# Probabilities turned in 32x32 blocks on VectorE and through DRAM in place of most TensorE transposes

## The chip, the cores and the metric

One core of a Trainium2 chip runs the whole program. The metric is the device time in microseconds, the median of the runs shown; lower is better.

## What is computed

Three stages, each on the output of the one before, all in float32 with 4 batches of 576 positions:

```python
# 1. attention, 8 heads of 64, each position sees itself and the 63 before it
scores = scale * q @ k^T;  attn = softmax(where(0 <= i - j < 64, scores, -1e9))
x = (attn @ v)                       # 4 x 576 x 512
# 2. gated layer with a spatial mix
h = relu(x @ w_in);  u, v = halves of h
v_s = w_spatial @ layernorm(v) + b_spatial
x = (u * v_s) @ w_out
# 3. four attention experts, causal, the best two per position by x @ w_gate
for e in range(4):
    a = softmax(causal(scale * (x @ wq[e]) @ (x @ wk[e])^T))
    out += gate[e] * (a @ (x @ wv[e])) @ wo[e]
```

## The kernel before, in words

A planner in the kernel file sets the order of all work. Each step is a node made with `N((engine, ns), emit, deps, alloc, use)`; `Planner.run` (L224) goes through time with the costs written at the nodes, gives each free engine the ready node with the lowest key and emits it at once. So each engine executes a fixed order, and at run time it waits in that order for the semaphores of what a step needs. The keys are one number per node in the long table `KEY` (L39), not derived from the node. When TensorE would go between full 128x128 products and the products on parts of its array, `SWITCH` is added to the key (L252). DMAs are nodes of SP (`load`, L511) and go through one hardware queue in order.

There are two planned phases.

Phase 1 holds stages 1 and 2. The first attention is done in 24 couples (`a_couple`, L581), a couple being two groups of 192 positions of a head pair. Per couple, TensorE makes the scores (`s_mm`, L612) into two PSUM banks, one for each head of the pair, each of three 128x128 blocks. Per bank, VectorE adds the mask and takes the extremum (L629), ScalarE does the exponential and the sum (L635), VectorE the reciprocal (L653), VectorE, GpSimd or ScalarE the scaling (L641, L643). Then TensorE transposes P three times (`p_t`, L647), a copy moves it from PSUM into `pt` (L656), and `pv` (L669) multiplies with V. The rings `pa` and `pt` hold four tiles of one head's P each (L497, L500). The second stage (`b_v`, `b_u`, `b_mix`) is woven between the couples: the first batch's couples run mostly ahead of it, those of the later batches beside it.

Phase 2 is the third stage. For each batch and each of two expert pairs, 8 pairs in all, `scores` (L1226) makes the causal scores of the query tiles I = 0 to 3 (128 I + 128 keys wide; 0 and 1 together) and of the tail tile 4. `unit` (L1278) does for one tile and one expert the mask and extremum (L1307), exponential (L1313), reciprocal (L1316) and scaling by the gate (L1317), then I + 1 transposes (`tr`, L1327) and a copy into `pg` (`tc_`, L1331). `c_pv` (L1351) multiplies with V, once for tiles 0 and 1 (group 0) and once for tiles 2 to 4 (group 1). `c_wo` (L1391) projects and stores. P tiles are five of 128x576 (L1070); projections of the next pair (`c_qk`, `c_v`) and the output projection are woven between the units (L1456 to L1466).

The masks are made at the start on VectorE and GpSimd (L450 to L470). Products of TensorE with an identity keep it busy at the start and wherever nothing else is ready (L515 to L523, 68 of them).

Of the kernel before, what the change touches and what calls it, by code (L numbers as in the profile page):

```python
# [8 lines left out]
F32 = mybir.dt.float32  # L9
# [13 lines left out]
N_XT = 5  # L23
N_VR = 3
N_W2 = 2
N_Q = 6
SWITCH = (51316.5562883, 56444.76665)
A_BIAS = 10098.0
C_BIAS = 162315.0
DVE_BIAS = (924.812225719, 2809.18155958)  # L30
POOL_BIAS = (605.73769693, 3223.06614942)
# [3 lines left out]
EFT = (348.130120865, 591.3127716)  # L35
# [6 lines left out]
    1e+09, 1e+09, 1e+09, 1e+09, 1e+09, 1e+09, 1e+09, 1e+09, 1e+09, 1e+09, 1e+09, 1e+09, 1e+09, -433949.337, -310768.212, -410360.675, -53326.873, -46012.043, -29718.587, 29893.476, 36423.798, 130640.442, 48760.892, -102410.634,  # L42
# [136 lines left out]
class Planner:  # L179

    LAT = 200.0, 165.0, 130.0, 75.0, 900.0
    ISSUE, WAY, RATE, FLIGHT = 475.0, 650.0, 360.0, 8

    DRAIN = (0.0, 145.0, 145.0, 92.0), (0.0, -78.0, 0.0, 0.0), (0.0, 0.0, -78.0, 0.0), (0.0, 0.0, 0.0, -92.0)

    CLASH, BEHIND = 1.0, 2200.0

    def __init__(self):
        self.nodes, self.free, self.prio = [], [1500.0, 2000.0, 2900.0, 7600.0, 560.0], 0.0
        self.moved, self.unit = [-1e9] * self.FLIGHT, 0
# [158 lines left out]
def attn_gmlp_moe_kernel(ctx: ExitStack, tc: tile.TileContext, kq0, qT, kT, v, w_in, wspT, b_sp, w_outT,  # L352
# [110 lines left out]
    for x in range(2):  # L463
        MASK[x, 1 - x] = m = const.tile([128, 128], F32, name=f"mix{x}")
        for y in range(2):
            pool.tensor_scalar(m[HALF[y]], (mask0, mask1)[x ^ y][HALF[y]], 1.0, 1.0, op0=ALU.mult, op1=ALU.mult)
# [757 lines left out]
    SC = {}  # L1224
# [292 lines left out]
```

## Time and profile before

| | us |
|---|---|
| median of 3 runs | 441.62 |
| lowest to highest | 441.45 to 443.12 |
| the profiled execution | 441.42 |
| its span, first to last instruction | 439.6 |
| TensorE products busy | 432.1 |
| VectorE busy | 288.6 |
| ScalarE busy | 275.8 |
| GpSimd busy | 90.0 |

Busy times are added over the span. The time of an execution holds some 1.8 us around its span. A float32 product is recorded as two instructions, a transpose as one. PEld is TensorE's loading of its stationary operand, which runs beside its products. An engine's idle time is put down to what it waited for last.

### The profile page before, as it was taken

What the parts mean: (1) busy time and instruction counts of PE and PEld (TensorE: products, weight loads), DVE (VectorE), ACT (ScalarE), POOL (GpSimd) and SP (SyncE); (2) the same over time, 40 slices, a digit from 0 to 9 for tenths busy, and PEclk for the clock granted to TensorE, in tenths of its full rate; (3) what the DMA queues carried; (4) which work ended last, traced back from release to release, by engine and by line L of the source; (5) the groups of instructions that cost most, each with busy time, mean ns of one, the idle gap of its engine ahead of it and who ended that gap; (6) DMA issues with size and microseconds to landing.
All of it is one profiled execution on the core that took longest, in us unless ns stands there. A gap on an engine that the chain in (4) does not pass through costs nothing.

```text
span 439.6 us, 10921 instructions
## 1 busy us (share of the span) xinstructions
PE 432.1 (98%) x4058; PEld 390.0 (89%) x4058; DVE 288.6 (66%) x1238; ACT 275.8 (63%) x883; POOL 90.0 (20%) x132
## 2 busy tenths in 40 slices
PE   8999999999999999999999999999999999999997
PEld 7988989998889989998999999999799978987775
DVE  4999998695787583354435444977654956498750
ACT  4899986787785273352433352867576748557873
POOL 4556754121041050001100120120012101110000
PEclk9999999999999999999999999999999999999999
DMA  8995614364145020121001000000020002000114
GB/s 269 339 343 151 238 51 154 96 205 120 38 108 147 1 73 0 49 73 49 1 1 50 0 1 1 0 2 2 1 97 1 1 1 98 1 0 2 49 51 143
DMA packets 31079, 33.11 MB, mean 75 GB/s; under 512 B 1905, under 2 KB 24689, under 8 KB 31026
## 3 DMA queue, kind: packets, MB, share of 16 engines
q1 hardware_dynamic: 31026, 32.41, 23.5%
q8 instruction: 32, 0.52, 0.5%
q14 instruction: 21, 0.17, 0.1%
HBM read 27.68 MB, written 4.72 MB: 74 GB/s over the span
## 4 chain that ended last, share of the span: by engine, by line
PE 84%; DVE 10%; ACT 3%; issue 1%; DMA 1%; POOL 1%; SPq 0%; DVEq 0%; POOLq 0%; ACTq 0%
PE bank L416 75%; PE bank L1329 5%; PE bank L647 4%; DVE p L1307 3%; DVE p L1300 2%; DVE p L1317 1%; ACT p L1313 1%; DMA kt<-in_kT_dram 1%; POOL p L1317 1%; DVE mc L1315 1%; DVE qk L440 0%; DVE mc L1316 0%; ACT pa L635 0%; DVE t2w L440 0%; DVE pa L629 0%
## 5 line engine op out<-in xcount | busy, mean ns | idle before, releaser
L416 PE MATMUL bank<-xh,w 128*128 128x288 f32 x512 | 109.5, 298 | 0.0
L416 PEld LDWEIGHTS bank<-xh,w 128*128 128x128 f32 x512 | 84.1, 188 | 1.4 <-issue 0.3
L416 PE MATMUL bank<-xl,w 128*128 128x288 f32 x256 | 75.5, 295 | 0.0
L416 PE MATMUL bank<-w,xh 128*128 128x512 f32 (+1 forms) x256 | 64.8, 343 | 0.0
L635 ACT ACTIVATE pa<-pa,mx 128x128 f32<-128x128 f32 x144 | 55.8, 393 | 12.7 <-DVE mx L629 12.6
L1313 ACT ACTIVATE p<-p,mc 128x256 f32<-128x256 f32 (+4 forms) x72 | 41.5, 577 | 15.5 <-DVE mc L1307 13.7
L416 PEld LDWEIGHTS bank<-xl,w 128*128 128x128 f32 x256 | 48.1, 188 | 0.4
L416 PEld LDWEIGHTS bank<-w,xh 128*128 128x128 f32 x256 | 43.0, 188 | 5.0 <-DVE mx L651 0.2
L416 PE MATMUL bank<-w,xl 128*128 128x512 f32 (+1 forms) x128 | 43.2, 338 | 0.0
L1317 POOL TENSOR_SCALAR p<-p,mc,fx 128x384 f32<-128x384 f32 (+4 forms) x22 | 14.6, 664 | 133.8 <-DVE mc L1316 66.8
L416 PE MATMUL bank<-wsp_h,vh 128*128 128x288 f32 x128 | 38.9, 304 | 0.0
L416 PE MATMUL bank<-wsp_l,vh 128*128 128x288 f32 x128 | 37.7, 294 | 0.0
L416 PE MATMUL bank<-wsp_h,vl 128*128 128x288 f32 x128 | 37.7, 294 | 0.0
L1307 DVE CUSTOM_DVE_ANT_0 p<-bank,cmask 128x512 f32<-128x512 f32 (+3 forms) x64 | 28.8, 487 | 4.8 <-PE bank L416 2.4
L629 DVE CUSTOM_DVE_ANT_0 pa<-bank,mask 128x128 f32<-128x128 f32 x120 | 28.2, 286 | 4.4 <-PE bank L416 4.3
L853 POOL TENSOR_TENSOR st<-st,nhalf 128x1 f32<-128x1 f32 (+1 forms) x20 | 11.8, 592 | 92.2 <-DVE st L852 56.6
L427 ACT ACTIVATE pg<-bank 128x512 f32<-128x512 f32 (+4 forms) x80 | 29.7, 438 | 0.7 <-PE bank L1329 0.2
L1329 PE MATMUL bank<-ident,p 128*128 128x128 f32 x192 | 27.2, 276 | 1.7 <-DVE p L1317 0.7
L427 ACT ACTIVATE pt<-bank 128x384 f32<-128x384 f32 x41 | 18.4, 486 | 15.8 <-PE bank L647 15.8
L635 ACT ACTIVATION_READ_ACCUMULATOR pa<-pa,mx 128x1 f32 x144 | 27.6, 192 | 0.0
L416 PEld LDWEIGHTS bank<-w,xl 128*128 128x128 f32 x128 | 24.1, 188 | 2.8
L1329 PEld LDWEIGHTS bank<-ident,p 128*128 128x128 f32 x192 | 21.6, 140 | 5.5 <-DVE p L1317 2.6
(193 smaller groups left out, 989.9 us busy)
## 6 DMA issues: line engine op xcount, KB each, us to landing
vt<-in_v_dram SPq DMA_DIRECT2D x12, 512.0 KB, 5.0
qa<-in_qT_dram SPq DMA_DIRECT2D x44, 96.0 KB, 4.4
out_dram<-ot SPq DMA_DIRECT2D x15, 256.0 KB, 2.1
y<-in_w_in_dram SPq DMA_DIRECT2D x7, 512.0 KB, 6.2
kt<-in_kT_dram SPq DMA_DIRECT2D x12, 288.0 KB, 5.3
y<-in_w_outT_dram SPq DMA_DIRECT2D x4, 512.0 KB, 4.2
y<-in_wspT_dram SPq DMA_DIRECT2D x2, 576.0 KB, 4.0
vt<-in_kq_dram SPq DMA_DIRECT2D x2, 384.0 KB, 3.8
```

The source lines that it names most:

```text
L416: pe.matmul(o, lhsT, rhs, start=start, stop=stop)
L427: act.activation(o, i, AF.Copy)
L629: dve.tensor_tensor_reduce(out=pa[:, j, :], in0=ps[:, j * 128:(j + 1) * 128], in1=mask(j), scale=-0.125, scalar=3.0e38, op0=ALU.add, op1=A ...
L635: act.activation(pa[:, j, :], pa[:, j, :], AF.Exp, bias=mx[:, j, 0:1], scale=-1.0, accum_out=mx[:, j, 1:2])
L647: pe.transpose(ps2[:, j * 128:(j + 1) * 128], pa[:, j, :], ident)
L853: a = N((POOL, 464), lambda e: pool.tensor_tensor(out=st[:m, 9:10], in0=st[:m, 8:9], in1=nhalf[:m], op=ALU.pow), [n1], use=[st])
L1300: dve.tensor_tensor_reduce(out=P[HALF[y], a0:a1], in0=ps[y][HALF[y], :HS], in1=cmask[HALF[y], 0:HS] if i == 0 else tmask[HALF[y]], scale=- ...
L1307: tops = [N((DVE, t_tt(L)), lambda _, ps=ps: dve.tensor_tensor_reduce(out=P[:, cs], in0=ps[:, cs], in1=cmask[:, 512 - L:512], scale=-0.125 ...
L1313: a = N((ACT, 284 + 0.87 * L), lambda e: act.activation(P[:, cs], P[:, cs], AF.Exp, bias=mc[:, 0:1], scale=-1.0, accum_out=mc[:, 2:3]), to ...
L1315: a = N((DVE, 70), lambda e: dve.tensor_scalar(mc[:, 3:4], mc[:, 2:3], 1e-9, None, op0=ALU.add), [a], use=[mc], prio=prio)
L1317: a = N({POOL: 328 + 0.832 * L, DVE: 90 + 0.52 * L}, lambda e: engs[e].tensor_scalar(P[:, cs], P[:, cs], mc[:, 3:4], fx[:, I, ev:ev + 1], ...
L1329: pe.transpose(ps[:, j * m:(j + 1) * m], P[:, c0 + j * 128:c0 + (j + 1) * 128], ident)
```

## The change

P of the last 16 couples of the first attention (`far`, from group 16 on) and of tiles 0 to 3 of all expert pairs but the last, (3, 1), is transposed in another way. The mask step writes P with its columns sorted by 32-column blocks; one VectorE instruction turns all 32x32 blocks of a tile in place; four DMAs write the four 32-partition strips to a DRAM tile, and a read (one, or two where a tile's experts lie apart) brings them back so that keys lie on partitions. The transposes on TensorE and the copies out of PSUM go for these. Near couples, the last pair and every tail tile keep them.

For this the P tiles become 128x768 for both heads of a couple (`pa` 4, `pt` 3 instead of 4) and 128x1024 in the second attention (6 instead of 5); `pg` is laid out in blocks of 32 queries; the scores' keys of far pairs are read in sorted order; the product with V of group 0 goes tile by tile. A mask `kmask` with sorted columns is made by GpSimd at the start. The tail tile's copy is split in two. The planner gets a table of the cost of going from each of five forms of product to each other one (transposes form a form of their own), other costs for some nodes, and a new `KEY` for every node. The program is built with a DMA scratch of 2048.

```diff
-SWITCH = (51316.5562883, 56444.76665)
+N_DT = 16
+NEAR = {(3, 1)}
+N_P = 6
+SWITCH = (508440.848706, 3824.76008776)
...
-    DRAIN = (0.0, 145.0, 145.0, 92.0), (0.0, -78.0, 0.0, 0.0), (0.0, 0.0, -78.0, 0.0), (0.0, 0.0, 0.0, -92.0)
+    DRAIN = ((0.0, 138.0, 137.0, 191.0, 0.0),
...
-                    key = n.prio + (SWITCH[self.phase] if e == PE and (n.form > 0) != (self.form > 0) else 0.0), n.nth
+                    key = n.prio + (SWITCH[self.phase] * self.DRAIN[self.form][n.form] if e == PE else 0.0), n.nth
...
+    for I in range(4):
+        L, c = 128 * I + 128, 64 * I * I + 64 * I
+        pool.tensor_copy(kmask[:, c:c + L].rearrange("p (k j c) -> p k j c", k=4, c=32),
+                         cmask[:, 512 - L:512].rearrange("p (j k c) -> p k j c", k=4, c=32))
...
-    r_pa = ring(p1, "pa", [128, 3, 128], F32, 4)
+    r_pa = ring(p1, "pa", [128, 768], F32, 4)
-    r_pt = ring(p1, "pt", [128, 3, 128], F32, 4)
+    r_pt = ring(p1, "pt", [128, 768], F32, 3)
+    r_dr = ring(dram, "dr", [4, 4, 32, 192], F32, 4)
...
+        far = n0 >= N_DT
...
+        if far:
+            a = N((DVE, 870), lambda e: dve.transpose(pa.t, pa.t), done, use=[pa], prio=prio, sbuf=True)
+            dr = r_dr.new()
+
+            def there():
+                for i in range(4):
+                    dma(dr[i].rearrange("k a w -> a k w"), pa[i * 32:(i + 1) * 32, :].rearrange("p (k w) -> p k w", k=4))
+
+            a = load(128 * 3072, 4, there, [a], alloc=[dr], use=[pa], prio=prio)
+            done = [load(128 * 3072, 1, lambda: dma(pt.t.rearrange("p (i w) -> p i w", i=4),
+                                                    dr.t.rearrange("i k a w -> (k a) i w")), [a], alloc=[pt], use=[dr], prio=prio)]
...
-                        mm(ps3[HALF[e], (3 * x + j) * 64:(3 * x + j + 1) * 64], vap(x, vi, e), pts[e][:, j, HALF[x]])
+                        mm(ps3[HALF[e], (3 * x + j) * 64:(3 * x + j + 1) * 64], vap(x, vi, e), prob(j, x, e))
...
-    r_p = Ring(None, 5, tiles=[p2.tile([128, S], F32, name=f"p{i}") for i in range(5)])
+    r_p = Ring(None, N_P, tiles=[p2.tile([128, 1024], F32, name=f"p{i}") for i in range(N_P)])
+    r_d2 = ring(dram, "d2", [4, 4, 32, 256], F32, 8)
...
+                return x.rearrange("p (j k c) -> p k j c", k=4, c=32) if perm else x
...
+    def far(b, pr, tiles):
+        prio = plan.prio - C_BIAS
+        scores(b, pr, tiles, prio)
+        w = sum(64 * I + 64 for I in tiles)
...
+        a = N((DVE, 68 + 4.16 * w), lambda e: dve.transpose(P[:, :4 * w], P[:, :4 * w]), done, use=[P], prio=prio, sbuf=True)
+        d2, grp = r_d2.new(), int(tiles[0] > 1)
...
+        def there():
+            for i in range(4):
+                dma(d2[i, :, :, :w].rearrange("k a w -> a k w"), P[i * 32:(i + 1) * 32, :4 * w].rearrange("p (k w) -> p k w", k=4))
+
+        def back():
+            src = d2[:, :, :, :w].rearrange("i k a w -> (k a) i w")
+            if grp == 0:
+                dma(pg.t, src)
+            elif w == 256:
+                dma(pg[:, 4:8].rearrange("p i e c -> p i (e c)"), src)
+            else:
+                for e in range(2):
+                    dma(pg[:, 0:4, e, 0:96], src[:, :, 96 * e:96 * e + 96])
...
+                    if grp == 0:
+                        for i in range(j, 2):
+                            c = 64 * i + e * 32 * (i + 1) + 32 * j
+                            mm(ps[e * 64:(e + 1) * 64, i * 128:(i + 1) * 128], v2[:, j, vs], pg[:, :, c:c + 32], j == 0, j == i)
+                        continue
+                    if j < 4:
+                        x = pg[:, a // 32:, e, j * 32:j * 32 + 32]
...
+        if (b, pr) not in NEAR:
+            us = [(1700, lambda: far(b, pr, [0, 1])), (760, lambda: c_pv(b, pr, 0)), (1200, lambda: far(b, pr, [2])),
+                  (1600, lambda: far(b, pr, [3])), (1600, lambda: unit(b, pr, 0, 4)), (2420, lambda: c_pv(b, pr, 1))]
+            return us
...
-    nc = _bacc.Bacc("TRN2", target_bir_lowering=False, num_devices=1)
+    nc = _bacc.Bacc("TRN2", target_bir_lowering=False, num_devices=1, dynamic_dma_scratch_size=2048)
```

## Rows read from the trace of the kernel before

**Rows 1.** Page, parts 1 and 2: busy time by engine; granted clock in 40 slices.
```profile
PE 432.1 (98%) x4058; PEld 390.0 (89%) x4058; DVE 288.6 (66%) x1238; ACT 275.8 (63%) x883; POOL 90.0 (20%) x132
...
PEclk9999999999999999999999999999999999999999
```
**Rows 2.** Busy time by stretch: from:to, length, each engine (instructions), clock, DMA share, GB/s.
```profile
0.00:66.00 66.00, 63.53 (x752) 56.46 (x756) 57.05 (x242) 56.24 (x192) 38.73 (x63) 1.00 0.71 232
66.00:200.00 134.00, 134.00 (x1460) 123.30 (x1453) 88.72 (x395) 83.03 (x306) 26.21 (x32) 1.00 0.30 87
...
275.00:430.00 155.00, 153.28 (x1264) 132.86 (x1261) 107.59 (x510) 105.81 (x314) 17.61 (x24) 1.00 0.06 22
```
**Rows 3.** Page, part 4: the chain that ended last, by engine.
```profile
PE 84%; DVE 10%; ACT 3%; issue 1%; DMA 1%; POOL 1%; SPq 0%; DVEq 0%; POOLq 0%; ACTq 0%
```
**Rows 4.** The same stretches, instructions on tile pt alone: PE, PEld, DVE, ACT.
```profile
66.00:200.00 134.00, 14.05 (x384) 12.24 (x384) 1.64 (x3) 12.91 (x29) 1.00 0.30 87
```
**Rows 5.** TensorE in order of time: start, duration, products around three transposes, first stage.
```profile
195.78 0.29 PE L416 MATMUL bank<-t1w,t1v 128*128 128x288 f32 x1
195.91 0.29 PE L416 MATMUL bank<-t2w,t2v 128*128 128x288 f32 x1
196.04 0.49 PE L647 MATMUL bank<-ident,pa 128*128 128x128 f32 x3
...
196.51 0.29 PE L416 MATMUL bank<-wsp_l,vh 128*128 128x288 f32 x1
```
**Rows 6.** TensorE in order of time around eight transposes, second attention.
```profile
346.71 0.30 PE L416 MATMUL bank<-xh,w 128*128 128x288 f32 x1
346.85 1.03 PE L1329 MATMUL bank<-ident,p 128*128 128x128 f32 x8
...
347.85 0.30 PE L416 MATMUL bank<-xl,w 128*128 128x288 f32 x1
```
**Rows 7.** Groups by line and shape: count, busy us, mean ns, idle before and its releasers.
```profile
L1329 PEld LDWEIGHTS bank<-ident,p 128*128 128x128 f32 x192 | 21.6, 140 | 5.5 <-DVE p L1317 2.6 <-POOL p L1317 1.5 <-DVE mc L1315 0.8
...
L427 ACT ACTIVATE pg<-bank 128x512 f32<-128x512 f32 x24 | 14.0, 597 | 0.4
...
L427 ACT ACTIVATE ot<-bank 128x512 f32<-128x512 f32 x17 | 9.9, 591 | 5.5 <-PE bank L416 4.3 <-ACT pg L427 0.8 <-ACT xh L427 0.5
...
L440 DVE TENSOR_TENSOR xl<-y,xh 128x576 fp32r<-128x576 f32 x10 | 7.9, 813 | 3.6 <-ACT xh L427 3.4
...
L416 PE MATMUL bank<-qk 64*128 64x512 f32 x48 | 7.2, 403 | 0.0
...
L1317 DVE TENSOR_SCALAR p<-p,mc,fx 128x512 f32<-128x512 f32 x13 | 7.1, 543 | 0.1
...
L757 POOL TENSOR_SCALAR y<-y 128x512 f32<-128x512 f32 x5 | 3.9, 786 | 2.9 <-DMA y<-in_w_in_dram 2.1 <-DVE wol L440 0.6 <-POOL woh L429 0.2
...
L416 PE MATMUL bank<-qk 64*128 64x128 f32 x48 | 3.8, 263 | 0.0
...
L440 DVE TENSOR_TENSOR w<-vt,w 128x1024 fp32r<-128x1024 f32 x3 | 3.7, 1226 | 1.1 <-ACT w L427 0.9
...
L440 DVE TENSOR_TENSOR wsp_l<-y,wsp_h 128x576 fp32r<-128x576 f32 x3 | 3.4, 1149 | 0.1
```
**Rows 8.** The stretch from 275 us, instructions on tile pg alone: PE, PEld, ACT, POOL.
```profile
275.00:430.00 155.00, 22.54 (x216) 13.95 (x216) 29.72 (x80) 0.00 (x0) 1.00 0.06 22
```
**Rows 9.** Loads of qa (issue ns and landing us, min/median/max), then landing of output stores.
```profile
L509 SPq DMA_DIRECT2D qa<-in_qT_dram x44: 327/413/1668, 3.1 to 132.5; - x44
...
DMA to landing us min/median/max: 1.9/4.4/8.3
...
DMA to landing us min/median/max: 1.9/2.3/4.3
```
**Rows 10.** Waits of SP's queue: us in total, times, longest.
```profile
SPq L509 <- ACT ot L427: 189.0, 12, 81.5
```
**Rows 11.** Page, part 3: the queue of all loads and stores; packets, MB, share of 16 engines.
```profile
q1 hardware_dynamic: 31026, 32.41, 23.5%
```

More of the change, by code (lines that the diff above doesn't have):

```diff
@@ L619, in mask @@
             return MASK[tuple(int(3 * g + j > 0) for _, _, g in grp)]
[L621 removed]
+        S_N[n0] = S_N[n0 + 1] = top = N((PE, 654), s_mm, kn + [Q_N[n0], Q_N[n0 + 1], S_N.get(n0 - 1)], alloc=bank, use=hk, prio=prio,
                                         form=1)
[L623 to L627 removed]
+        done, first, turned = [], [], []
@@ L628, in s_top @@
+        for e2, ps in enumerate(bank):
+            mx = r_mx.new()
+            def s_top(_, ps=ps, e2=e2, mx=mx):
                 for j in range(3):
-                    dve.tensor_tensor_reduce(out=pa[:, j, :], in0=ps[:, j * 128:(j + 1) * 128],
-                                             in1=mask(j), scale=-0.125, scalar=3.0e38,
+                    dve.tensor_tensor_reduce(out=at(j, e2), in0=sq(ps[:, j * 128:(j + 1) * 128]),
+                                             in1=sq(mask(j)), scale=-0.125, scalar=3.0e38,
@@ L639, in s_norm @@
                 if e == ACT:
                     for j in range(3):
-                        act.activation(pa[:, j, :], pa[:, j, :], AF.Copy, scale=mx[:, j, 3:4])
-                else:
-                    engs[e].tensor_tensor(out=pa.t, in0=pa.t, in1=mx[:, :, 3:4].to_broadcast([128, 3, 128]), op=ALU.mult)
-            def p_t(_, pa=pa, ps2=ps2):
-                for j in range(3):
-                    pe.transpose(ps2[:, j * 128:(j + 1) * 128], pa[:, j, :], ident)
-            a = N((DVE, 606), s_top, [top], alloc=[pa, mx], use=[ps], prio=prio)
+                        act.activation(at(j, e2), at(j, e2), AF.Copy, scale=mx[:, j, 3:4])
+                elif far:
+                    o = pa.t.rearrange("p (k e j c) -> p k e j c", k=4, e=2, j=3)[:, :, e2]
+                    engs[e].tensor_tensor(out=o, in0=o, in1=mx[:, None, :, 3:4].to_broadcast([128, 4, 3, 32]), op=ALU.mult)
+                else:
+                    o = pa[:, e2 * 384:(e2 + 1) * 384].rearrange("p (j c) -> p j c", j=3)
+                    engs[e].tensor_tensor(out=o, in0=o, in1=mx[:, :, 3:4].to_broadcast([128, 3, 128]), op=ALU.mult)
@@ L650, in a_couple @@
+            a = N((DVE, 606), s_top, [top] + first, alloc=[mx] + ([] if e2 else [pa]), use=[ps] + ([pa] if e2 else []), prio=prio)
+            first.append(a)
             a = N((ACT, 1160), s_exp, [a], use=[pa, mx], prio=prio)
@@ L914, in gv @@
         def gv(g):
-            return g.t.rearrange("p a b -> p (a b)")[:, :HS]
+            return g[:, :HS]
         def gate(o):
@@ L1053, in attn_gmlp_moe_kernel @@
     r_qk = ring(p2, "qk", [128, 4 * S], F32R, 3)
-    PG1 = [p2.tile([128, 4, 2, 320], F32, name=f"pg1{i}") for i in range(2)]
+    PG1 = [p2.tile([128, 10, 2, 128], F32, name=f"pg1{i}") for i in range(2)]
     Z_N = {}
@@ L1063, in zeros @@
     def zeros(pr):
-        zero(("p", pr), [PG1[pr][HALF[1 - x], 3, :, x * 64:(x + 1) * 64] for x in range(2)], 200.0)
+        zero(("p", pr), [PG1[pr][HALF[1 - x], 2 * x:2 * x + 2, :, 96:128] for x in range(2)], 200.0)
     r_v2 = ring(p2, "v2", [128, 4, 256], F32, 2)
@@ L1261, in scores @@
             return
-        ps, pp = [r_sc.new(), r_sc.new()], [r_p.new(), r_p.new()]
+        ps = [r_sc.new(), r_sc.new()]
+        pp = [r_p.new() for _ in range(2 if (b, pr) in NEAR else 1)]
         def go(_):
@@ L1267, in go @@
                 w = 128 * I + 128
-                three([p[:, c:c + w] for p in ps], (w - 128, w - 128), 0, w)
+                three([p[:, c:c + w] for p in ps], (w - 128, w - 128), 0, w, (b, pr) not in NEAR)
                 c += w
-        a = N((PE, 92 + sum(3 * t_mm(128 * I + 128) for I in tiles)), go, deps, alloc=ps + pp + gets, use=[qk], prio=prio, form=3)
+        a = N((PE, sum(3 * t_mm(128 * I + 128) for I in tiles)), go, deps, alloc=ps + pp + gets, use=[qk], prio=prio, form=3)
         started(a)
@@ L1276, in scores, with put, as4 @@
             c += 128 * I + 128
+    def far(b, pr, tiles):
+        prio = plan.prio - C_BIAS
+        scores(b, pr, tiles, prio)
+        w = sum(64 * I + 64 for I in tiles)
+        done = []
+        for I in tiles:
+            sn, banks_, pp, c0 = SC[b, pr, I]
+            P, L = pp[0], 128 * I + 128
+            off = 64 if I == 1 else 0
+            for e in range(2):
+                mc, ps = r_mc.new(), banks_[e]
+                ev = 2 * pr + e
+                fx, _, fn = FX[b]
+                def put(P=P, e=e, I=I, off=off):
+                    c = off + (32 * I + 32) * e
+                    return P[:, :4 * w].rearrange("p (k w) -> p k w", k=4)[:, :, c:c + 32 * I + 32]
+                def as4(x):
+                    return x.rearrange("p (k w) -> p k w", k=4)
+                a = N((DVE, t_tt(L)), lambda _, ps=ps, c0=c0, L=L, put=put, as4=as4, mc=mc, I=I: dve.tensor_tensor_reduce(
+                    out=put(), in0=as4(ps[:, c0:c0 + L]), in1=as4(kmask[:, 64 * I * I + 64 * I:64 * I * I + 64 * I + L]), scale=-0.125, scalar=3.0e38,
+                    op0=ALU.add, op1=ALU.min, accum_out=mc[:, 0:1]), [sn], alloc=[mc], use=[ps, P], prio=prio)
+                a = N((ACT, 284 + 0.87 * L), lambda _, put=put, mc=mc: act.activation(
+                    put(), put(), AF.Exp, bias=mc[:, 0:1], scale=-1.0, accum_out=mc[:, 2:3]), [a], use=[P, mc], prio=prio)
+                a = N((DVE, 70), lambda _, mc=mc: dve.tensor_scalar(mc[:, 3:4], mc[:, 2:3], 1e-9, None, op0=ALU.add), [a], use=[mc], prio=prio)
+                a = N((DVE, 75), lambda _, mc=mc: dve.reciprocal(mc[:, 3:4], mc[:, 3:4]), [a], use=[mc], prio=prio)
+                done.append(N({POOL: 328 + 0.832 * L, DVE: 190 + 0.52 * L}, lambda en, put=put, mc=mc, fx=fx, I=I, ev=ev: engs[en].tensor_scalar(
+                    put(), put(), mc[:, 3:4], fx[:, I, ev:ev + 1], op0=ALU.mult, op1=ALU.mult), [a, fn],
+                    use=[P, mc, fx], prio=prio, sbuf=True))
+        a = N((DVE, 68 + 4.16 * w), lambda e: dve.transpose(P[:, :4 * w], P[:, :4 * w]), done, use=[P], prio=prio, sbuf=True)
+        d2, grp = r_d2.new(), int(tiles[0] > 1)
+        pg = PG[b, pr, grp]
+        def there():
[8 more added lines that the diff above has]
+            else:
+                for e in range(2):
+                    dma(pg[:, 0:4, e, 0:96], src[:, :, 96 * e:96 * e + 96])
+        a = load(128 * 16 * w, 4, there, [a], alloc=[d2], use=[P], prio=prio)
+        PG_N[b, pr, grp].append(load(128 * 16 * w, 2 if tiles == [2] else 1, back, [a] + PG_N[b, pr, grp][:1], use=[d2, pg], prio=prio))
```

86 lines of the change are left out of this document (54 added, 32 removed), and 167 rows, old and new, of the table KEY.

## The prediction, made before the changed kernel ran

> **What bounds the kernel now.** I read the page's busy shares first: TensorE works 98% of the span, VectorE 66%, ScalarE 63%, GpSimd 20%, and the granted clock is at its upper level in every slice [rows 1, 2]. Next the busy times by stretch [rows 2]: from 66 to 200 us TensorE is busy 134.00 of 134 us, and from 275 to 430 us 153.28 of 155. VectorE has 88.7 and 107.6 us there, 66% and 69%. Only in the first 66 us do VectorE and ScalarE run at 86% and 85%, and TensorE's busy time there holds warming products, so those 66 us answer to other engines. Last the chain of waits, which puts 84% of the span on TensorE and 10% on VectorE [rows 3]. So from 66 us on a TensorE instruction that goes gives its time back, unless what replaces it comes late.
>
> **What goes from TensorE.** The far couples are the last 16 of 24; each has 6 transposes at L647, 96 in all. Their products with P are 24 records a couple, and the stretch from 66 to 200 us holds 384, which is 16 couples [rows 4]. Of the second attention's transposes at L1329 a pair has 24: 20 for tiles 0 to 3 and 4 for the tail tile. Seven pairs lose their 20, which makes 140.
> The price of one is read where TensorE has no gap. Where TensorE goes from product to product, those of 288 columns start 0.13 us apart [rows 5]; with three transposes between them, the product before the block starts at 195.91 and the second after it at 196.51. That is 0.60 us for two products and three transposes: 0.60 - 2 x 0.131 = 0.338, or 113 ns each, the slow first product behind them included. A block of eight makes 347.85 - 346.71 = 1.14 us [rows 6], less 0.262 = 0.88, or 110 ns each. So 96 x 0.113 = 10.8 us in the first stage and 140 x 0.110 = 15.4 us in the second: **26.2 us**.
>
> **What TensorE gets.** The first product group of the second attention (tiles 0 and 1) is cut into six products of 128 columns instead of two of 256 and two of 128: the same 768 columns with two more starts, 0 to 0.1 us a pair, 0.4 us in all. The scores of far pairs and all products with far P read their moving operand in runs of 32 columns. No row shows TensorE doing so. The nearest is a ScalarE copy written in runs (597 ns for 512 columns) against a plain one (591 ns) [rows 7], which is no loss. The other end is half speed: the far tiles' scores are 48 records each of four widths, the widest 7.2 us and the narrowest 3.8 us busy [rows 7], some 21 us for the four, so up to 19 us for seven pairs. I take nothing, as the row says, and keep the other end for the upper half of the range.
>
> **What VectorE gets.** 16 turns of 768 columns, and for each of 7 pairs two of 768 and one of 1024: 30 and 7 instructions. The trace has no such instruction. Fast end: the single-input scale of 512 columns takes 543 ns [rows 7], so 0.81 us for 768 and 1.09 us for 1024 in proportion. Slow end: the two-input subtraction of 1024 columns takes 1.23 us, the one of 576 columns 0.81 us [rows 7], so about 0.96 us for 768. I take the slow end, a column of 4-byte words each cycle: 30 x 0.96 + 7 x 1.23 = 37.4 us. By stage: 16 x 0.96 = 15.4 us on 88.7, less the three copies of this stretch that were VectorE's (1.6 us [rows 4]), makes 102.5 of 123 us, 83%. In the second attention 7 x 3.15 = 22.0 us on 107.6 makes 129.6 of 155 - 15.4 = 139.6 us, 93% if nothing moves elsewhere. But the scaling at L1317 can move: 13 of those of 512 columns alone are 7.1 us on VectorE, while GpSimd has 17.6 of 155 us.
> Row first: one transpose costs TensorE 110 ns here [rows 6], the turn replacing six some 0.96 us. The Trainium skill ("VectorE: DVE Perf Modes", The three transpose paths, and Rules for kernel authors) advises TensorE for a full 128x128 transpose when the result may go to PSUM, and gives 311 ns for VectorE's on 2-byte data. Taken per block, that would be an estimate of 236 x 0.311 = 73 us on VectorE instead of 37. The trace does not show which holds; the rival with slow turns below is this case, worked out from rows.
>
> **What ScalarE loses.** The copies out of PSUM: 29 of the pt copies between 66 and 200 us (12.9 us [rows 4]) and 56 of the 80 pg copies (29.7 x 56/80 = 20.8 us [rows 8]). It was off the path, but it can now take copies that VectorE has. The tail tile's copy is split in two (8 times, at most one more copy's 0.6 us each [rows 7]), hidden there. The mask made at the start is four GpSimd copies, 1280 columns together, 0 to 2.0 us by a scale of 512 columns (0.79 us [rows 7]); GpSimd has 27 free us of the first 66 [rows 2], so I take nothing.
>
> **What the transfers add.** 16 + 7 x 3 = 37 round trips through DRAM. A couple issues four writes of 98 KB and one read of 393 KB; a pair 12 writes and 4 reads. That is 192 more instructions on SP's queue at 0.33 to 0.41 us [rows 9], some 70 us in a queue that has waited 189 us on output copies alone [rows 10]. One round trip: four issues 1.5 us, landing 2.1 us (out stores land in 1.9 at least, 2.3 median [rows 9]), one issue 0.4 us, the read about 3.5 us (qa loads 1.9 at least and 4.4 median, beside large loads [rows 9]). Sum 7.5 us, where a block of three transposes and a copy took some 0.34 + 0.60 us [rows 5, 7]. The bytes: 16 x 2 x 0.39 + 7 x 2 x 1.31 = 31 MB on 32.4 MB that took 23.5% of the engines' span [rows 11]; twice that is no bound.
> The wait is new in two places. On SP a read-back waits for its writes to land; behind it stand the q, k and v loads of later couples, and later the output stores. On TensorE the product with P waits for the read; behind that stands everything in its order. What hides it: in the first stage P has as many buffers for whole couples as it had for half ones, and the projections and spatial mix stand between couples (one couple in 134/16 = 8.4 us); in the second, six P buffers and the next pair's projections. The last pair, with nothing behind it, keeps its transposes. Exposed wait: 0 to 7.5 us a trip; I take 2 us for all 37, as the stretch in question has more cover than one trip is long.
>
> **The new order** replaces each priority, so it can't be priced step by step. Waits of TensorE's weight loads for transposes are 5.5 us in all in the second attention [rows 7]; seven eighths of them lose their place, and come back as waits for the read. The changed planner also charges each change between kinds of product by a measured table and far more strongly; I take 2 us gained, 0 to 5. Against it stands VectorE at 80 to 93%: the first 66 us, where it is at 86%, show TensorE idle 2.5 of 66 us, 3.7% [rows 2]; on 139.6 us that is 5.2 us at most, I take 3.
>
> **The sum**, from the profiled execution's 441.42 us (span 439.6; the median of the runs is 441.62, so the two agree): 441.4 - 10.8 - 15.4 + 0.4 + 2 + 3 - 2 = 418.6 us.
>
> **Rivals.**
> *VectorE becomes the bound of the second attention.* If nothing moves to GpSimd and VectorE gets no further than the 86% of the first 66 us, its 129.6 us need 150.7: that stage gives 4.3 us instead of 15.4, and the time is 441.4 - 10.8 - 4.3 = 426, to 433 with some exposed trips. For it: 69% already. Against: free GpSimd and ScalarE.
> *Turns at half that rate, no change.* A subtraction of 576 columns beside GpSimd's work took 1.15 us [rows 7], 2 ns a column. At that rate the turns of a pair are 5.1 us; the stage has 107.6 + 35.8 = 143.4 us, at 86% 167 us, 12 over its present 155: 441.4 - 10.8 + 12 = 442.6. The Trainium skill's advice above would lead here. Against: that row is the exception beside 0.81 us for the same shape.
> *Round trips stand open, slower.* SP executes in order, so a read-back that waits for its writes holds the next trip's writes and the loads, the read lands late, and TensorE stands before the product. It decides from 26.2/37 = 0.7 us exposed per trip; at 1.0 us each the time is 441.4 - 26.2 + 37 = 452. For it: qa loads landed up to 8.3 us after issue [rows 9]. Against: such loads had large ones ahead of them, and the second attention has hardly any loads.
> *The order gains more.* All trips hidden, no loss on VectorE, 5 us less changing of kinds: 441.4 - 26.2 - 5 = 410, down to 405.
>
> **How the numbers follow.** The forecast 418.6 (411 to 424) has 0.58; VectorE as bound (424 to 433) 0.17; the better order (405 to 411) 0.07; no change 0.05; slower (over 444) 0.13. The range 409 to 437 holds the first two, part of the third, and the gap between the second and no change, about 0.8; strided reading at half speed (418.6 + 19 = 437.6) is its upper end. Faster by over 0.5%, about what a measurement can tell here, is 0.82, within it 0.05, slower 0.13.
>
> **What would show it.** Right: TensorE's transposes fall from 344 records to 108 and its busy share stays at 96% or more; turns of 768 columns near 0.96 us; VectorE near 325 us busy, ScalarE near 240. Wrong: idle TensorE ahead of products with P released by DMA (round trips); idle ahead of the scores' successors released by VectorE (the bound); score products longer than 403 ns at 512 columns [rows 7] (strided reading); a granted clock below its upper level, since a long halt can cost that too.

## The result, and the profile after

The changed kernel takes 417.38 us (median of 4 runs, 416.30 to 418.14) against 442.25 us of the kernel before, run beside it (441.45 to 443.12). The ratio is 0.9435, with a 95% interval of 0.9404 to 0.9467: 5.6% faster. The forecast was 418.6 us, the range 409 to 437, faster 0.82. The profiled execution took 418.14 us, its span 416.4 us.

The page of the changed kernel, answering to [rows 1, 3, 11]: busy time by engine, granted clock in 40 slices, the queue of all loads and stores, the chain that ended last.

```profile
PE 406.7 (98%) x3854; PEld 368.3 (88%) x3854; DVE 294.8 (71%) x1213; ACT 247.4 (59%) x824; POOL 127.2 (31%) x191
...
PEclk9999699999999999999999999999999999999999
...
q1 hardware_dynamic: 75570, 63.35, 52.7%
...
PE 82%; DVE 6%; DMA 4%; ACT 3%; POOL 2%; issue 2%; SPq 1%; DVEq 0%; POOLq 0%; ACTq 0%
```

TensorE is still the bound, with the same 98%, and has 25.4 us less to do (432.1 to 406.7). VectorE got only 6 us more in all, though 37.6 us of turns are among it; GpSimd got 37 us more (90.0 to 127.2), and ScalarE 28 us less. One slice of the granted clock, the fifth, is below the upper level.

Busy time by stretch, changed kernel, answering to [rows 2] (the last one ends at 410 us, since the whole is shorter):

```profile
0.00:66.00 66.00, 61.17 (x696) 53.79 (x697) 51.02 (x250) 55.73 (x210) 33.62 (x62) 0.95 0.76 237
66.00:200.00 134.00, 133.56 (x1455) 123.04 (x1454) 91.04 (x374) 77.92 (x287) 41.74 (x51) 1.00 0.65 183
...
275.00:410.00 135.00, 134.22 (x1129) 116.87 (x1128) 113.03 (x482) 84.02 (x257) 35.52 (x48) 1.00 0.59 166
```

From 66 us on TensorE stays full; VectorE is at 68% in the first attention and at 84% in the second. The new weak place is ahead of 66 us.

Groups by line and shape, changed kernel (count, busy us, mean ns, idle before), answering to [rows 7]; the turns have no counterpart there.

```profile
L695 DVE STREAM_TRANSPOSE pa<-pa 128x768 f32<-128x768 f32 x16 | 15.4, 969 | 2.7 <-ACT pa L666 2.6
L1360 DVE STREAM_TRANSPOSE p<-p 128x768 f32<-128x768 f32 x14 | 13.5, 967 | 0.4 <-POOL p L1357 0.3
L1360 DVE STREAM_TRANSPOSE p<-p 128x1024 f32<-128x1024 f32 x7 | 8.7, 1239 | 0.0
L688 PE MATMUL bank<-ident,pa 128*128 128x128 f32 x48 | 7.7, 276 | 1.4 <-POOL pa L672 1.4
L1432 PE MATMUL bank<-ident,p 128*128 128x128 f32 x52 | 7.6, 279 | 0.3 <-DVE p L1420 0.3
L421 PE MATMUL bank<-qk 64*128 64x512 f32 x48 | 7.1, 399 | 0.0
...
L1449 PE MATMUL bank<-ident,p 128*64 128x128 f32 x8 | 2.3, 282 | 0.3 <-POOL p L1420 0.3
```

The transposes left are 48 + 52 + 8 = 108. The turns take 15.4 + 13.5 + 8.7 = 37.6 us. The scores with 512 columns, 42 of whose 48 records belong to far pairs and so read in runs of 32 columns, take 399 ns, against 403 before.

Issues of the changed kernel's transfers (count, KB each, median us from issue to landing):

```profile
dr<-pa SPq DMA_DIRECT2D x64, 96.0 KB, 2.3
pt<-dr SPq DMA_DIRECT2D x16, 384.0 KB, 4.1
d<-p SPq DMA_DIRECT2D x56, 96.0 KB, 2.5
...
pg<-d SPq DMA_DIRECT2D x7, 512.0 KB, 5.1
```

The longest of TensorE's waits in the changed kernel (us in total, times, longest); none is put down to a read of P:

```profile
PE bank L421 <- issue: 1.8, 1, 1.8
PE bank L421 <- DVE ident L451: 1.5, 1, 1.5
PE bank L688 <- POOL pa L672: 1.4, 1, 1.4
PE bank L421 <- DVE mx L654: 0.6, 2, 0.4
```

One of them is such a read all the same, of a far couple's P. The longer of the two waits in the last line stands ahead of a product that reads `pt` and not `mx`:

```profile
93.53 0.92 PE L421 MATMUL bank<-pt,vt 128*64 128x64 f32 x24 [0.44 <-DVE mx L654]
```

The read back of P issued at 88.52 us landed 4.9 us later, at 93.4 us, just as this wait ended. In a second profile of the changed kernel, used below, the same wait is 0.96 us, up to 90.94 us, and a read issued at 87.2 us landed 3.6 us later, at 90.8 us. So of the 37 trips one was seen to stand open, by 0.4 to 1.0 us.

To split the gain by stage one instruction serves as a mark: the last product with `woh` (count, duration, first and last start), which ends the second stage. First the kernel before, then the changed one.

```profile
L416 PE MATMUL bank<-w,woh x96: 274/283/288, 225.8 to 255.8; 128*128 128x256 f32 x64, 128*128 128x260 f32 x32
```

```profile
L421 PE MATMUL bank<-w,woh x96: 274/283/285, 222.8 to 252.8; 128*128 128x256 f32 x64, 128*128 128x260 f32 x32
```

The first two stages gained 3.0 us only, where the forecast had 10.8 us of transposes there; what follows the mark shrank from 439.6 - 255.8 = 183.8 to 416.4 - 252.8 = 163.6, by 20.2 us, where it had 15.4. By this profile the total was right and the split was not. The experiments ask why.

### The profile page after: what moved, and what is told of

It reads as the page before. It is cut to its first block, busy times and chain, and to the rows that moved or that the text cites. A ratio compares the mean times of both kernels' runs of the same rounds, so it can differ in the third digit from the quotient of the medians.

```text
span 416.4 us, 10959 instructions
## 1 busy us (share of the span) xinstructions
PE 406.7 (98%) x3854; PEld 368.3 (88%) x3854; DVE 294.8 (71%) x1213; ACT 247.4 (59%) x824; POOL 127.2 (31%) x191
## 4 chain that ended last, share of the span: by engine, by line
PE 82%; DVE 6%; DMA 4%; ACT 3%; POOL 2%; issue 2%; SPq 1%; DVEq 0%; POOLq 0%; ACTq 0%
PE bank L421 80%; DMA y<-in_w_in_dram 1%; PE bank L1432 1%; DMA d<-p 1%; DVE pa L654 1%; DMA pg<-d 1%; DVE p L1403 1%; SPq L520 1%; PE bank L688 1%; ACT pa L660 1%; POOL xl L445 1%; ACT p L1353 0%; DVE p L1360 0%; ACT pa L666 0%; ACT xh L432 0%
## 5 line engine op out<-in xcount | busy, mean ns | idle before, releaser
L421 PE MATMUL bank<-xh,w 128*128 128x288 f32 x512 | 108.0, 297 | 0.0
L660 ACT ACTIVATE pa<-pa,mx 128x128 f32<-128x128 f32 x144 | 55.9, 397 | 4.3 <-DVE mx L654 4.2
L421 PEld LDWEIGHTS bank<-w,xh 128*128 128x128 f32 x256 | 44.0, 190 | 5.9 <-DVE mc L1355 0.4
L1357 POOL TENSOR_SCALAR p<-p,mc,fx 128x256 f32<-128x256 f32 (+3 forms) x35 | 22.6, 652 | 79.7 <-DVE mc L1356 21.6
L1353 ACT ACTIVATE p<-p,mc 128x128 f32<-128x128 f32 (+3 forms) x56 | 31.0, 557 | 15.4 <-DVE mc L1350 10.8
L421 PE MATMUL bank<-wsp_h,vh 128*128 128x288 f32 x128 | 37.9, 296 | 0.0
L432 ACT ACTIVATE xh<-bank 128x192 fp32r<-128x192 f32 (+1 forms) x35 | 12.5, 381 | 24.6 <-PE bank L421 24.4
L1350 DVE CUSTOM_DVE_ANT_0 p<-bank,kmask 128x128 f32<-128x128 f32 (+3 forms) x56 | 25.6, 483 | 0.3
L666 ACT ACTIVATE pa<-pa,mx 128x128 f32<-128x128 f32 x69 | 22.5, 394 | 5.5 <-DVE mx L679 4.4
L965 DVE TENSOR_TENSOR y<-bank,ut 128x288 f32<-128x288 f32 x24 | 10.7, 450 | 21.2 <-PE bank L421 20.8
L421 PE MATMUL bank<-qk 64*128 64x288 f32 (+4 forms) x288 | 25.1, 319 | 0.1
```

The costliest lines, as they stand in the source:

```text
L421: pe.matmul(o, lhsT, rhs, start=start, stop=stop)
L432: act.activation(o, i, AF.Copy)
L660: act.activation(at(j, e2), at(j, e2), AF.Exp, bias=mx[:, j, 0:1], scale=-1.0, accum_out=mx[:, j, 1:2])
L666: act.activation(at(j, e2), at(j, e2), AF.Copy, scale=mx[:, j, 3:4])
L965: dve.tensor_tensor(out=o, in0=ps[:, :HS], in1=u[:, d, tk], op=ALU.mult)
L1350: a = N((DVE, t_tt(L)), lambda _, ps=ps, c0=c0, L=L, put=put, as4=as4, mc=mc, I=I: dve.tensor_tensor_reduce(out=put(), in0=as4(ps[:, c0:c0 ...
```

## The experiments

**The transposes by themselves.** The changed kernel in its own order, with 236 transposes of the identity, which nobody reads, put back on TensorE ahead of the far products.

```diff
         def pv(_):
+            for _i in range(6 if far else 0):
+                pe.transpose(ps3[:, 384:512], ident, ident)
...
         def go(_):
+            for _i in range(0 if (b, pr) in NEAR else 6 if grp == 0 else 14):
+                pe.transpose(ps[:, 384:512], ident, ident)
```

> The changed kernel with the removed transposes given back to TensorE as work that nobody reads: 6 transposes of a constant ahead of each far couple's product with P, 6 and 14 ahead of the two product groups of each far pair, 236 in all, into a free part of the same PSUM bank. The order of all other instructions on every engine is that of the changed kernel, and nothing waits for them. Theory (TensorE's time is the gain, 110 to 113 ns a transpose): 417.4 + 26 = 443 us, 440 to 446, with about 10 us more before 253 us of the changed kernel's trace and 15 more behind. Rival (the new order and the freed ScalarE made the gain, and the transposes had lain in gaps): under 425 us.

Measured: 443.40 us (443.14 to 443.94), ratio to the kernel before 1.0051 (1.0031 to 1.0071). So 26.0 us come from taking 236 transposes off TensorE (27.3 us against the 416.11 us of four later runs of the changed kernel), and all the rest of the change together (turns, trips, order, GpSimd's share) costs 443.40 - 441.47 = 1.9 us against the kernel before on that chip. Its mark, and then that of a second profile of the changed kernel, in which the clock stayed at its upper level throughout as it did here:

```profile
L421 PE MATMUL bank<-w,woh x96: 274/283/285, 231.5 to 261.4; 128*128 128x256 f32 x64, 128*128 128x260 f32 x32
```

```profile
L421 PE MATMUL bank<-w,woh x96: 274/283/285, 220.3 to 250.2; 128*128 128x256 f32 x64, 128*128 128x260 f32 x32
```

261.4 - 250.2 = 11.2 us for 96 transposes, 117 ns each. The spans are 441.4 and 413.6 us, so behind the mark 180.0 - 163.4 = 16.6 us for 140, 119 ns each. And against the kernel before, with transposes in both: 261.4 - 255.8 = 5.6 us lost ahead of the mark, 183.8 - 180.0 = 3.8 us won behind it. That is where the split went: all of the change but the transposes costs the first two stages 5.6 us and pays back 3.8 in the third. This run does not tell the order, the trips and the turns apart; 2.6 us of both numbers are filling products that moved from one side of the mark to the other (see what stays open, below).

**One part alone.** First the second attention's part, with stages 1 and 2 as in the kernel before; then the first attention's part, with the third stage as before. The first is written from the kernel before, and gets the third stage of the changed one; the second is written from the changed kernel.

```diff
+NEAR = {(3, 1)}
...
+    def far(b, pr, tiles):
...
+        if (b, pr) not in NEAR:
```

```diff
-NEAR = {(3, 1)}
+NEAR = {(b, p) for b in range(4) for p in range(2)}
```

Keys and the planner's rules of the restored phase are those of before as well; in the first of the two the couples' code too.

> The first two stages word for word in the order of the kernel before, no far couple; the third stage as in the changed kernel. By the two traces the time from the last folded product of the second stage to the end fell by 20 us, and the time up to it by 3. Theory: 442 - 20 = 422 us, 419 to 425. If the third stage gained only what its 140 transposes are worth: 427 us. If the third stage's gain hangs on the new first stage: over 432 us.

Measured: 422.20 us (421.60 to 422.59), ratio 0.9565 (0.9547 to 0.9583).

> The first two stages as in the changed kernel, the third in the order of the kernel before with all its transposes on TensorE. Theory (the stages add up, and the first gained only 3 us because its new order lost some 8 us in the first 66 us): 442 - 3 = 439 us, 436 to 441. By the prediction's own term for the 96 transposes: 431 us.

Measured: 435.91 us (435.22 to 436.79), ratio 0.9878 (0.9857 to 0.9899): 5.6 us faster where 3 was expected, a little outside. The second part alone gives 19.3 us, and 19.3 + 5.6 = 24.9. Both together gave 442.25 - 417.38 = 24.9 us in the first measurement and 441.71 - 416.11 = 25.6 in the later one: they add up. The mark of the run with the first part alone:

```profile
L424 PE MATMUL bank<-w,woh x96: 274/283/285, 220.6 to 250.6; 128*128 128x256 f32 x64, 128*128 128x260 f32 x32
```

250.6, not 252.8 us, with the same order up to there, so the 3.0 us of the first profile was itself 2 us too low. By the second profile the stages up to the mark gained 255.8 - 250.2 = 5.6 us, and what follows it 183.8 - 163.4 = 20.4. Busy time by stretch (columns as in [rows 2]) in the two profiles of the changed kernel, the first with all engines and the later one with TensorE alone:

```profile
38.00:47.00 9.00, 5.81 (x98) 4.74 (x90) 6.27 (x43) 6.15 (x30) 4.06 (x5) 0.72 0.49 136
47.00:55.00 8.00, 8.00 (x39) 6.35 (x32) 7.40 (x22) 7.95 (x28) 3.84 (x4) 0.89 0.68 181
```

```profile
38.00:47.00 9.00, 6.86 (x114) 1.00 0.54 146
47.00:55.00 8.00, 8.00 (x43) 1.00 0.79 214
```

TensorE has a hole there in both. In the first the granted clock fell to its lower level for a part of these stretches (0.72 and 0.89 on average), and the mark came 2.6 us later.

**The order of before.** The first phase of the changed kernel, far couples included, with the keys, the switch price and the node costs of the kernel before.

```diff
-SWITCH = (508440.848706, 3824.76008776)
+SWITCH = (51316.5562883, 3824.76008776)
...
-EFT = (590.178157957, 1602.10028593)
+EFT = (348.130120865, 1602.10028593)
```

> The changed kernel with the first two stages ordered by the keys, the switch rule and the node costs of the kernel before; the far couples stay far (a turn takes the key of the scaling before it, the writes that of the transpose, the read that of the copy). Theory (the first 66 us lost 7.7 us because TensorE was kept on couples by the new switch price while VectorE lagged): the loss goes, 417.4 - 7.7 = 410 us, 407 to 414, if the old order also covers the round trips. Rival (the new order is needed to cover the round trips of the far couples): 417 us or more, with idle TensorE ahead of their products with P.

Measured: 445.71 us (444.43 to 447.59), ratio 1.0102 (1.0068 to 1.0137). The expectation of 410 us fell; the other order is 28 us worse under this change, all of it ahead of the mark, which comes at 283.4 us; behind it are 445.8 - 283.4 = 162.4 us, no more than in the changed kernel. TensorE's waits in it:

```profile
PE bank L422 <- DMA vt<-in_v_dram: 6.6, 2, 5.2
PE bank L422 <- DVE mx L655: 6.4, 5, 3.6
PE bank L422 <- DVE t1v L446: 3.0, 1, 3.0
```

Its stretches (columns as above):

```profile
22.00:44.00 22.00, 17.96 (x262) 15.16 (x260) 17.49 (x76) 18.82 (x69) 13.36 (x13) 0.92 0.86 283
44.00:66.00 22.00, 19.19 (x167) 16.10 (x171) 17.92 (x72) 18.09 (x63) 11.13 (x12) 0.77 0.49 155
66.00:88.00 22.00, 16.64 (x193) 13.45 (x182) 17.48 (x87) 16.68 (x62) 9.43 (x10) 0.93 0.60 174
...
198.00:220.00 22.00, 16.79 (x156) 15.46 (x155) 8.94 (x25) 6.17 (x15) 4.42 (x6) 0.92 0.21 66
```

The products wait for v loads and for VectorE, with holes up to 220 us, and the granted clock is below its upper level in each of these stretches (0.77 to 0.93 on average), which is in the 28 us too. Already ahead of 66 us it loses time, where there are few far couples, so not all of the 28 us is a matter of the trips; this run does not separate the two.

**Products that wait for no trip.** Products with far P read a tile filled once with 1/128, so that turned P is left out of the result; turns, writes and reads still run.

```diff
+    fk = const.tile([128, 320], F32, name="fk")
+    pool.memset(fk, 0.0078125)
...
-                return pt.t.rearrange("p (i e j c) -> p i e j c", i=4, e=2, j=3)[:, 2 * x:2 * x + 2, e, j, :]
+                return fk[:, 0:128].rearrange("p (i h c) -> p i h c", i=2, h=2)[:, :, 0, :]
```

The products of the second attention are changed in the same way.

> The changed kernel in its own order, but the products that should read the far P back from DRAM read a tile that is filled once with 1/128: left out is that the turned P enters the result; the turns, the writes to DRAM and the reads back all still run. So TensorE waits for no round trip. Theory (the order covers the round trips, what is left of them costs 2 us at most): 415.4 to 417.4 us, that is 0 to 2 us under the changed kernel's 417.4. Rival (the trips stand open by a part of a microsecond or more each, 37 of them, and the change hides a larger loss): 410 us or less. If products are now faster than the tail that still has to wait for VectorE, same.

Measured: 416.47 us (414.94 to 417.19), ratio 0.9423 (0.9397 to 0.9449). The changed kernel has 417.38 us in the first four runs and 416.11 in four later ones, so this is no different: what stands open of the round trips, the one wait of 0.4 to 1.0 us shown above, is too little to tell in the time. With the constant tile the products of far couples have no wait ahead of them. My 2 us for 37 trips was too much. Writes and reads still hold the queue in this run, so it does not show what they cost the loads behind them.

**Each turn twice.** VectorE does every turn two times, in the second attention too, which undoes it; P enters the products not turned.

```diff
-            a = N((DVE, 870), lambda e: dve.transpose(pa.t, pa.t), done, use=[pa], prio=prio, sbuf=True)
+            a = N((DVE, 870), lambda e: [dve.transpose(pa.t, pa.t) for _ in range(2)], done, use=[pa], prio=prio, sbuf=True)
```

> The changed kernel in its own order, with every turn in 32x32 blocks on VectorE done twice (so P goes back untouched, and the result is that of P not turned). VectorE gets 15.4 us more in the first attention and 13.5 + 8.7 = 22.2 us more in the second, where it is busy 113.0 of 135.0 us: 135.2, its whole time. Theory (VectorE has slack now, and the change stopped short of its bound): the first stage absorbs its 15.4 us, the second attention loses a third to a half of its 22.2, 7 to 11 us: 425 us, 421 to 430. Rival (VectorE is on the path already): about all of 22.2 us and part of 15.4, 440 us or more. Second rival (the turns lie far ahead of their products, so it costs nothing): 419 us or less.

Measured: 433.09 us (432.28 to 434.14), ratio 0.9805 (0.9779 to 0.9832): 15.7 us more than the changed kernel (17.0 by its later runs) for 38.0 us on VectorE, and above the 421 to 430 us of the theory. Busy time by stretch:

```profile
0.00:66.00 66.00, 61.32 (x712) 54.11 (x713) 52.63 (x252) 56.84 (x213) 34.57 (x62) 1.00 0.77 237
66.00:200.00 134.00, 131.34 (x1437) 120.79 (x1437) 102.65 (x383) 77.47 (x284) 41.13 (x50) 1.00 0.65 183
...
253.20:430.70 177.50, 165.42 (x1322) 144.03 (x1320) 147.12 (x561) 94.58 (x290) 41.23 (x62) 0.98 0.47 131
```

Its mark is at 253.2 us, 3.0 us behind the second profile of the changed kernel: the first stage takes 12 of its 15 us without loss. Behind the mark 177.5 - 163.4 = 14.1 of the 22 us are lost, more than the third to a half that was expected. Of these, 12.1 - 4.3 = 7.8 us are more idle time of TensorE; the rest is a longer busy time, with the granted clock at 0.98 on average. So the rival that VectorE becomes the bound is not true of the changed kernel, but near: at 84% it has little left in the second attention.

**A longer trip, and the queue held.** In the first of two runs the bytes are copied once more from DRAM to DRAM ahead of each read. In the second the same copy stands behind the read, followed by a copy of 256 bytes that waits for it, so that the read does not stand behind the copy, and the queue is held. The lines of the first attention, the longer trip and then the held queue:

```diff
+                dma(x.rearrange("i k a w -> (i k a) w"), dr.t.rearrange("i k a w -> (i k a) w"))
-                dma(pt.t.rearrange("p (i w) -> p i w", i=4), dr.t.rearrange("i k a w -> (k a) i w"))
+                dma(pt.t.rearrange("p (i w) -> p i w", i=4), x.rearrange("i k a w -> (k a) i w"))
```

```diff
                 dma(pt.t.rearrange("p (i w) -> p i w", i=4), dr.t.rearrange("i k a w -> (k a) i w"))
+                dma(x.rearrange("i k a w -> (i k a) w"), dr.t.rearrange("i k a w -> (i k a) w"))
+                dma(DZ, x.rearrange("i k a w -> (i k a) w")[0:1, 0:64])
```

> The changed kernel in its own order; ahead of each read back the same bytes are copied once more from DRAM to DRAM by the same queue, so that each of the 16 trips of the first attention and the 28 reads of the second come later by some 3 us at least, and the queue holds everything behind them for as long. Theory (the order gives the trips more slack than they need): 417.4 to 421 us. Rival (the trips are just covered, what is added to them stands open): 16 + 7 or more trips of 3 us each: 69 us, 480 us; by half of them, 450 us.

Measured: 508.57 us (506.03 to 511.85), ratio 1.1537 (1.1472 to 1.1603). The theory of much slack fell: 91 us are lost. TensorE's waits and then those of SP's queue:

```profile
PE bank L421 <- DMA pg<-dy: 36.0, 7, 11.5
PE bank L421 <- DMA pt<-dx: 27.1, 9, 6.3
```

```profile
SPq L522 <- DMA dy<-d: 74.2, 21, 4.4
SPq L522 <- DMA dx<-dr: 54.1, 16, 5.4
```

Now TensorE waits long for reads of P, what the changed kernel hardly does. Whether by each trip's own length or by the queue, which was held 128 us, the second run tells:

> As the run with the longer trip, but the copy from DRAM to DRAM stands behind the read back instead of ahead of it, and a copy of 256 bytes behind that waits until it has landed: the queue is held for the same 4 us at each trip, while the trip itself is as long as in the changed kernel. Theory (what cost 91 us there is the queue: it takes its transfers in order, so all loads and trips behind a wait come later): nearly as slow, 480 to 510 us. Rival (there each product waited for its own longer trip): 417 to 430 us. Between them, the gap says how much is of each.

Measured: 538.87 us (537.15 to 543.64), ratio 1.2230 (1.2159 to 1.2300). TensorE's waits and SP's:

```profile
PE bank L421 <- DMA pg<-d: 47.1, 6, 16.5
PE bank L421 <- DMA pt<-dr: 26.8, 8, 4.6
```

```profile
SPq L523 <- DMA dy<-d: 89.7, 21, 6.2
SPq L523 <- DMA dx<-dr: 70.8, 16, 6.2
```

It is slower still, above the expected 510, though its trips are shorter than in the run before: in the first attention the writes land 3.2 us after their issue and the reads 4.9 (medians; 2.3 and 4.1 in the changed kernel), where the run before has 2.4, 3.9 for the copy and 3.5. The queue was held 160 us, and 122 us were lost, three quarters; in the run before 91 of 128 us, seven tenths. And the longest wait for a read here, 16.5 us, is three times what the reads take to land (3.6 to 5.4 us by median in the second attention), so that read was issued late. So the time goes with the wait on the queue rather than with the trip of one product: a wait there makes the later trips and loads late. How much of the loss is that alone is not shown. Both runs also move 15.5 MB more, and both lose clock: it is 0.929 and 0.882 on average, and the same 3854 records are busy 425.7 and 437.2 us, against 406.7 in the changed kernel. And no run has a longer trip that holds no queue. In the changed kernel the queue waits for its own writes too, ahead of the reads:

```profile
SPq L520 <- DMA dr<-pa: 15.3, 15, 3.2
...
SPq L520 <- DMA d<-p: 13.6, 11, 3.3
```

Those 28.9 us are covered as far as the products with P go, within what the run with the constant tile can tell. Whether they delay loads was not tried.

**The hole at 38 to 47 us.** One swap in TensorE's order: a couple's product with V, which the next wide products need, ahead of the scores of a later couple. It ran twice; the second time with the changed kernel on the same chip.

```diff
-        n.emit(e)
+        if n.nth == 454:
+            self.held = n
+        else:
+            n.emit(e)
+            if n.nth == 332:
+                self.held.emit(PE)
```

> The changed kernel with one swap in TensorE's order alone: at about 42 us the products of one couple's P with its values, which the first wide products of the next stage wait for, run ahead of the scores of the next couple, which wait for a load. Theory (the new order lost its first microseconds to the hole of TensorE between 38 and 47 us and to the lower granted clock behind it): the hole gets 1 to 2 us shorter, and the lower clock costs up to 2 us less: 413.5 to 416 us. Rival (what is won there is lost at the next wait for a load): 417.4 us within 0.5.

> The changed kernel once more, on the same chip as the two others of this call, to compare with the swap: 416 to 418.2 us, as before. Its profile also shows whether the lower granted clock between 38 and 47 us comes with every execution of it (then 0.7 again) or not (then near 1.0, at about the same time).

> The changed kernel with the one swap at 42 us, beside the changed kernel on one chip. If the swap is worth what it seemed (1.6 us): 414.5 to 416.3 us, and below the changed kernel's runs. If the two overlap as a whole, the swap does nothing that can be told.

Measured: with the swap 415.75 us (415.29 to 416.30), and the second time 415.75 (415.38 to 416.59); the changed kernel beside it 416.11 (415.40 to 417.98). That is no difference to be told. In the profile of the second run with the swap the halts behind 41 us are 0.53 and, ahead of scores that wait for a load of `kt`, 0.28 us, where the changed kernel beside it has 0.70: what it wins at one wait is lost at the next. The repeated profile, shown above, has the hole without the lower clock. So the clock is no part of every execution, and the hole is.

## Why the prediction was right, point by point

- *The bound* held: from 66 us on TensorE is busy 133.56 of 134 and 134.22 of 135 us, as [rows 2] had it.
- *The transposes, 26.2 us*: 26.0 us by the medians, 27.3 against the later runs, and 11.2 + 16.6 = 27.8 by the marks of two profiles at the same clock. The prices of 113 and 110 ns, read from [rows 5, 6], came out as 117 and 119, so the term was a little low. The price between two products is what an instruction in a full stream costs; its record alone (276 ns) would have given 65 us.
- *The extra products, 0.4 us, and strided reading, 0*: the scores at 399 ns beside 403 [rows 7], and the products of 320 columns with P at 436 beside 435, settle that reading runs of 32 columns costs nothing, so the upper end of the range, 437, was not called for.
- *The turns, 37.4 us*: 37.6. The slow end, read from a two-input subtraction, was right to 0.01 us: 0.97 us for 768 columns, 1.24 for 1024. The rival with turns at half rate falls. It was the case to which the Trainium skill ("VectorE: DVE Perf Modes", The three transpose paths, and Rules for kernel authors) leads with its advice to leave full transposes to TensorE and its 311 ns. By the trace one block of 128x128 costs VectorE 0.97/6 = 0.16 us, and the measurement decides. TensorE's own price is lower still, but TensorE was full and VectorE was not.
- *VectorE's loss, 3 us*: not seen; past the start, TensorE's waits for VectorE are some 0.5 us in the first profile and 1.2 in the second. VectorE ended at 294.8 us, not near 325, because some 31 us of its other work went to GpSimd and ScalarE. The scaling in the second attention is 11.0 + 3.1 us of VectorE, where it was 22.9: 35 of the far tiles' are GpSimd's at L1357 (22.6 us), where it had 21 at L1317. The scaling in the first attention is 4.4 + 2.2 us, where it was 13.6, and copies to `pt` and `xh` are 0.9, where they were 8.2; the rest is in small pieces. The text had said that the scaling can move, and then left it out of the forecast of 325. ScalarE at 247.4 us is near the forecast 240.
- *The trips, 2 us*: the term was too large: one trip stood open, by 0.4 to 1.0 us, and the constant tile does not change the time. The rival that they stand open put the point of decision on the length of a trip and named the queue as the reason. The queue was right: held for some 4 us at each trip, it costs 91 to 122 us, the lower clock in it.
- *The new order, 2 us gained*: this is the step that failed in size and place. All that is not transposes was to cost 0.4 + 2 + 3 - 2 = 3.4 us and cost 1.9. But it is 5.6 us lost ahead of the mark and 3.8 us won behind it. The stage sums 10.8 and 15.4 were right as prices (11.2 and 16.6), and hidden by that. That the total came within 1.2 us is in part luck: of the terms of that sum, the 3 us for VectorE, most of the 2 us for the trips and the 2 us to be won by the order were not seen, and the 1.9 us that were measured come from elsewhere. I had weighed the order as a gain alone, by its dearer changes between kinds and by 5.5 us of waits ahead of the transposes. Those 5.5 us are the weight loads', which run beside the products; the products at L1329 themselves waited 1.7 us before. And I had not asked what it does to the first 66 us, where other engines bound the work.
- *What stays open*: a part of both numbers is work that moved across the mark. Of the 68 products with the identity, which nobody reads, the kernel before has the last twelve (24 records) right behind the mark, ahead of the next product that counts:

```profile
256.02 2.84 PE L416 MATMUL bank<-ident 128*128 128x128 f32 x24
258.62 0.49 PE L416 MATMUL bank<-w,xh 128*128 128x260 f32 x2
```

In the new order all 68 run ahead of it. The run with the transposes put back (count, duration, first and last start):

```profile
L421 PE MATMUL bank<-ident x136: 275/275/580, 1.5 to 37.8; 128*128 128x128 f32 x136
```

So 258.62 - 256.02 = 2.6 us of the 5.6 lost and of the 3.8 won are the same. Of the 5.6 us, 1.4 us more is idle time of TensorE ahead of the mark (3.8 us with the transposes put back, 2.5 before): the hole at 38 to 47 us is 2.2 us, and the kernel before has a wait of 1.0 us at 59 us that is gone. The other 1.6 us was not located. Of the 3.8 us won, 5.0 - 3.9 = 1.1 us is less idle of TensorE behind the mark (its busy time there is 178.8 of 183.8 us before and 176.1 of 180.0 with the transposes put back), and the 2.6 us are nearly all the rest. The run with the second part alone still has the 24 records behind the mark, and takes 420.8 - 255.7 = 165.1 us there, 1.7 us more than the changed kernel: gone, they save less than their own length. So what the new order wins behind the mark by itself is some 1 to 2 us.

## What to carry to other kernels

Price an instruction that goes from a full engine by the distance between its neighbours in order of time, and price its replacement on another engine by the nearest row with the same number of columns. Where a replacement goes by DRAM, look at what else stands in the queue behind its wait, and not only at the length of the trip. And when the order changes with it, split the result at a mark that both kernels have, or a right total hides two wrong parts; and count on each side of the mark the products that only fill time. Where a wait is put down to an engine that the waiting instruction does not need, look for a transfer that landed just then.

## What the runs showed of the hardware that was not expected

A turn of 128x1024 float32 columns in 32x32 blocks takes 1.24 us on VectorE and one of 768 columns 0.97 us, in place. From these two, 256 columns more cost 0.27 us, some 1.05 ns each. That is the slow one of the two ends that were forecast.

The granted clock's fall behind the hole is not a matter of the program alone. In the first profile TensorE stood for 1.44 and 1.75 us, and the clock was at its lower level for a part of the time that follows: the product of 24 records at 44.20 us took 1.55 us. In the second, with halts of 1.44 and 0.70 us, the same product took 0.92 us. The second profile, TensorE in order of time:

```profile
40.37 0.88 PE L688 MATMUL bank<-ident,pa 128*128 128x128 f32 x6 [1.44 <-POOL pa L672]
41.95 1.00 PE L421 MATMUL bank<-kt,qa 64*64 64x128 f32 x24 [0.70 <-DVE mx L679]
42.88 0.92 PE L421 MATMUL bank<-pt,wol 128*64 128x64 f32 x24
```

The length of the halts alone does not decide it: both runs with the swap have halts of 1.44 and 0.53 us there, and the granted clock from 38 to 47 us is 0.81 on average in the first and 1.00 in the second. What does is not settled.
